# Transposing q and k of batches 1 to 3 by VectorE in 32x32 blocks, on data loaded as runs of 32 values

## Chip, cores and metric

One core of a Trainium2 chip. The metric is the device time of one execution in microseconds (us), lower is better. Before the change it is 926.97 us, the median of three runs (926.3 to 927.1).

## What is computed

```python
def _attn_ref(q, k, v):                       # 4 batches, 8 heads, 576 tokens, head size 64
    scores = q @ k.T / 8
    # heads 0 to 3 see the last 32 tokens (local), heads 4 to 7 every 32nd token before (strided)
    attn = softmax(where(mask, scores, -1e9))
    return attn @ v

def reference(...):
    x = attn_out.transpose(0, 2, 1, 3).reshape(2304, 512)
    h = relu(x @ w_in)                        # 512 -> 2048
    x = (s * h * h + b) @ w_out               # 2048 -> 512
    return ((x @ w_a) * (x @ w_b)) @ w_o2     # 512 -> 1536 -> 512
```

All inputs and the output are float32. The matmuls of the two MLPs run as three passes over a high and a low half of each operand (`PASSES`, line 153).

## The kernel before

**Chunks and steps.** The first MLP runs over five chunks of tokens, n = 0 to 4 (line 896). Chunk 0 holds the first 128 tokens of all four batches; chunk n from 1 on holds the other 448 tokens of batch n-1. A chunk takes 16 steps, one for each f of the 2048 hidden columns in blocks of 128. A step is, on TensorE, 12 matmuls `h` (`h_mm`, line 586), 12 matmuls `acc` for the f of two steps earlier (`o_mm`, line 614), and then a piece of the attention for the next chunk (`attend`, line 817). So TensorE sees `h`, `acc`, a short piece, `h`, `acc`, a short piece. After each `h`, ScalarE makes the ReLU and the high half of its square, VectorE the square and the low half (lines 599 to 610).

**The attention of the next chunk.** While chunk n-1 runs, the attention for chunk n is made by six generators: four `local` (line 238; two pairs of heads, each in a part of 4 and a part of 3 blocks of 64 tokens) and two `strided` (line 299; two pairs of heads). `plan` (line 804) says at which step each generator does its next part. For `local`: load q and k two steps ahead; transpose (step 0); load v, scores and first half of the softmax (step 1); second half (step 2); transpose the probabilities, `ppt` (step 3); multiply by v, `po`, and split the result into the halves of x (step 4). A `local` begins every 4 steps, so its step 0 falls together with step 4 of the one before. `strided` does the same over 8 steps, with the load three steps ahead.

**Transposes of q and k before.** Rows of 64 values are loaded, tokens on partitions (lines 249 and 307 to 311). TensorE transposes them against an identity into PSUM (`pst`, line 96, called from 259, 317 and 325), ScalarE copies PSUM into `qkT` or `sqkT` (lines 260, 318, 332). A `local` part of 4 blocks takes 5 such matmuls, a part of 3 blocks 4, a `strided` 10.

**Rooms.** `qkT` and the transposed probabilities `pT` share one buffer (tag `lT`), `sqkT` and `spT` another (tag `sT`); the loaded `sqk` shares a third with the probabilities `spt` (tag `sn`). Each has one buffer: the next user waits until the last reader is done.

**Order.** The order on each engine is set by a scheduler from the dependencies and its own simulation; TensorE's order is fixed by hand (`in_order`, line 85). All loads of the attention and of the weights go through the queue of SP, in order. The weights of the second MLP are converted meanwhile, a piece at a time (`convert_w2`, line 633, `raw`, lines 129 to 139).

The order of the passes matters at the first step of a chunk:

```python
for kk in range(KD):              # kk: block of 128 columns of x, blocks 0 and 1 from `local`
    for a, c in PASSES:           # ((0, 0), (0, 1), (1, 0)); c = 1 is the low half of x
        mm(ph, lhsT=wi[f][:, a, kk, :], rhs=x_t[n][:, c, kk, 0:T], ...)
```

Of the kernel before, what the change touches and what calls it, by code (L numbers as in the profile page):

```python
# [8 lines left out]
F32 = mybir.dt.float32  # L9
# [3 lines left out]
AF = mybir.ActivationFunctionType  # L13
# [5 lines left out]
P = 128  # L19
# [6 lines left out]
def sparse_attention_two_mlps(  # L26
# [14 lines left out]
    nc = tc.nc  # L41
    B, H, S, D = q.shape
# [3 lines left out]
    STR = 32  # L46
    HL = H // 2
# [24 lines left out]
    ps_a = ctx.enter_context(tc.tile_pool(name="ps_a", bufs=3, space=PSUM))  # L72
# [4 lines left out]
    sp = att.enter_context(tc.tile_pool(name="sp", bufs=1, side="right"))  # L77

    ident = const.tile([P, P], F32, name="ident")
# [15 lines left out]
    def mm_t(*args):  # L95
        last_pe[:] = [nc.tensor.transpose(*args).ins]  # L96
# [65 lines left out]
    QT = 64  # L162
    WK = QT + STR
    RG = 4
    NG = STR // RG
    NI = S // STR
    I0 = TF // STR
    IS = NI - QT // RG
    NK = NI * RG
# [64 lines left out]
    def window(src, bb, head, t0, nt):  # L234
        at = src[bb, head, t0:S, :]
        return bass.AP(at.tensor, at.offset, [[D, WK], [QT * D, nt], [1, D]])

    def local(bb, n, pair, t0, nt):

        nq, nk = nt * QT, nt * QT + STR  # L240
        mq, mk = (P, nk // 3) if nk % 3 == 0 else (nq // 2, nk // 2)
        cq, ck = nq // mq, nk // mk
        nu = -(-nt // 2)
        tl = lambda shape, name: lp.tile(shape, F32, tag=name, name=name)
        qn, kn = tl([P, 2, 2, D], "qn"), tl([P, 3, 2, D], "kn")
        for h in range(2):
            for dst, src, a, m in ((qn, q, t0, mq), (kn, k, t0 - STR, mk)):
                z = t0 + nq
                nc.sync.dma_start(
                    out=dst[:m, 0:(z - a) // m, h],  # L250
                    in_=src[bb, 2 * pair + h, a:z, :].rearrange("(c p) d -> p c d", p=m),
                )
        yield
        qkT = lp.tile([P, 9 * QT], F32, tag="lT", name="qkT")
        qT, kT = qkT[:, 0:nq], qkT[:, nq:nq + nk]
        for src, m, c, dst, eng in ((qn, mq, cq, qT, 0), (kn, mk, ck, kT, 0)):
            ps = ps_a.tile([P, c, m], F32, tag="a", name="pst")
            for i in range(c):
                mm_t(ps[:, i], src[:m, i].rearrange("p h d -> p (h d)"), ident[:m, :m])
            nc.scalar.activation(out=dst.rearrange("p (c m) -> p c m", m=m), in_=ps, func=AF.Copy)  # L260
        yield
        vn = tl([WK, 4, 2, D], "vn")
        for h in range(2):
            nc.sync.dma_start(out=vn[:, 0:nt, h], in_=window(v, bb, 2 * pair + h, t0 - STR, nt))
        pss = [ps_a.tile([P, nu, WK], F32, tag="a", name="pss") for _ in range(2)]

        def put(alone):
            for j in range(2 * nu if alone else nt):
                i = min(j, nt - 1) * QT
                for h in range(2):  # L270
                    hr = slice(h * D, (h + 1) * D)
                    mm(
                        pss[h][j % 2 * QT:(j % 2 + 1) * QT, j // 2],
                        lhsT=qT[hr, i:i + QT], rhs=kT[hr, i:i + WK],
                        start=alone, stop=(alone or j >= nt - 2),
                    )

        pt = tl([P, 2, nu, WK], "lpt")
        yield from softmax(pt, pss, lmask, put, n == 1)
        yield  # L280
        ppt = ps_a.tile([WK, 2 * nu, P], F32, tag="a", name="ppt")
        for i in range(2 * nu):
            mm_t(ppt[:, i, :], pt[:, i // nu, i % nu], ident)
        pT = lp.tile([WK, 2, nu * P], F32, tag="lT", name="pT")
        nc.scalar.activation(out=pT.rearrange("p h t -> p (h t)"), in_=ppt.rearrange("p i t -> p (i t)"), func=AF.Copy)
        yield
        po = ps_a.tile([P, nq], F32, tag="a", name="po")
        for j in range(nt):
            for h in range(2):
                mm(  # L290
                    po[h * D:(h + 1) * D, j * QT:(j + 1) * QT],
                    lhsT=vn[:, j, h, :], rhs=pT[:, h, j * QT:(j + 1) * QT],
                    start=True, stop=True,
                )
        xt, c0 = x_tile(n), t0 - TF
        split(xt[:, 0, pair, c0:c0 + nq], xt[:, 1, pair, c0:c0 + nq], po)
        yield

    def strided(bb, n, pair):

        NC, NH = (S - IS * STR) // P, 3
        MK = S // (2 * NH)
        room = sp.tile([P, NC + 2 * NH, 2, D], F32, tag="sn", name="sqk")
        sq, sk = room[:, 0:NC], room[:MK, NC:]
        for h in range(2):
            head = HL + 2 * pair + h
            nc.sync.dma_start(
                out=sq[:, :, h], in_=q[bb, head, IS * STR:S, :].rearrange("(c p) d -> p c d", p=P)
            )
            nc.sync.dma_start(  # L310
                out=sk[:, :, h], in_=k[bb, head].rearrange("(c p) d -> p c d", p=MK)
            )
        yield
        qkT = sp.tile([P, NG, QT + NK], F32, tag="sT", name="sqkT")
        ps = ps_a.tile([P, NC * P], F32, tag="a", name="pst")
        for c in range(NC):
            mm_t(ps[:, c * P:(c + 1) * P], sq[:, c].rearrange("p h d -> p (h d)"), ident)
        nc.scalar.activation(
            out=qkT[:, :, 0:QT].rearrange("p g (i r) -> p g i r", r=RG),
            in_=ps.rearrange("p (i g r) -> p g i r", r=RG, g=NG), func=AF.Copy,  # L320
        )
        for half in range(2):
            ps = ps_a.tile([P, NH * MK], F32, tag="a", name="pst")
            for c in range(NH):
                mm_t(
                    ps[:, c * MK:(c + 1) * MK], sk[:, half * NH + c].rearrange("p h d -> p (h d)"),
                    ident[:MK, :MK],
                )
            ih = NI // 2
            dst = qkT[:, :, QT:].rearrange("p g (r i) -> p g r i", r=RG)[:, :, :, half * ih:(half + 1) * ih]  # L330
            src = ps.rearrange("p (i g r) -> p g r i", r=RG, g=NG)
            nc.scalar.activation(out=dst, in_=src, func=AF.Copy)
        yield
        sv = sp.tile([NK, NG, 2, D], F32, tag="sv", name="sv")
        for h in range(2):
            vr = v[bb, HL + 2 * pair + h].rearrange("(i g r) d -> r i g d", r=RG, g=NG)
            for r in range(RG):
                nc.sync.dma_start(out=sv[r * NI:(r + 1) * NI, :, h], in_=vr[r])  # L338
        nu = NG // 2
        pss = [ps_a.tile([P, nu, NK], F32, tag="a", name="pss") for _ in range(2)]  # L340

        def put(alone):
            for g in range(NG):
                for h in range(2):
                    hr = slice(h * D, (h + 1) * D)
                    mm(
                        pss[h][g % 2 * QT:(g % 2 + 1) * QT, g // 2],
                        lhsT=qkT[hr, g, 0:QT], rhs=qkT[hr, g, QT:],
                        start=alone, stop=(alone or g >= NG - 2),
                    )  # L350

        pt = sp.tile([P, 2, nu, NK], F32, tag="sn", name="spt")
        yield from softmax(pt, pss, smask, put, False)
        yield
        skip = QT - IQ * RG
        pT = sp.tile([NK, 2, NG, IQ * RG], F32, tag="sT", name="spT")
        for h in range(2):
            ppt = ps_a.tile([NK, nu, 2, QT], F32, tag="a", name="ppt")
            for u in range(nu):
                mm_t(ppt[:, u].rearrange("p j t -> p (j t)"), pt[:, h, u], ident)  # L360
            src = ppt.rearrange("p u j t -> p (u j) t")[:, :, skip:]
            nc.scalar.activation(out=pT[:, h], in_=src, func=AF.Copy)
        yield
        po = ps_a.tile([P, TR], F32, tag="a", name="po")
        pg = po.rearrange("p (i g r) -> p g i r", r=RG, g=NG)
        for g in range(NG):
            for h in range(2):
                mm(
                    pg[h * D:(h + 1) * D, g], lhsT=sv[:, g, h],
                    rhs=pT[:, h, g].rearrange("p (i r) -> p i r", r=RG), start=True, stop=True,  # L370
                )
        xt = x_tile(n)
        split(xt[:, 0, HL // 2 + pair, 0:TR], xt[:, 1, HL // 2 + pair, 0:TR], po)
        yield
# [506 lines left out]
    for what in ORDER.split():  # L881
        name, of = what[:-1], int(what[-1])
# [104 lines left out]
    for pair in range(NP2):  # L987
        acc = [ps_acc.tile([P, DM], F32, tag="acc", name="acc2") for _ in range(TB2 // P)]
        later_x = []
        for g in range(NG2):  # L990
            i = pair * NG2 + g
# [112 lines left out]
```

## Time and profile before

| | us |
|---|---|
| median of 3 runs | 926.97 |
| the profiled execution, as timed | 926.5 |
| its span in the profile | 924.7 |
| TensorE matmul busy | 911.6 (99%) |
| VectorE busy | 615.5 (67%) |
| ScalarE busy | 418.5 (45%) |
| share of the span in the chain that ended last, TensorE | 89% |

The profile shows one execution. TensorE's busy time includes overlap of consecutive matmuls, so its starts are a better measure of a step than its durations. In the trace's timeline, a row merges equal instructions that follow each other: start, the time they cover, engine, line, operation, output and inputs, count. "Idle before" is the engine's idle time just before, with what ended it. Stage boundaries: chunk 1 begins at 138.4 us, chunk 2 at 233.9, chunk 3 at 328.7, chunk 4 at 422.9.

### The profile page before, as it was taken

To read this page: it belongs to the slowest core of one execution; us is meant where nothing else is said; L and a number is where in the kernel's file an instruction comes from. 1 tells how busy PE (TensorE), PEld (TensorE's weight loads), DVE (VectorE), ACT (ScalarE), POOL (GpSimd) and SP (SyncE) were. 2 spreads that over 40 slices of the span, in tenths; PEclk is the share of its full clock that TensorE was granted. 3 is DMA by queue.
4 is the path that set the end of the run, shared out by engine and by line. 5 is a ranking of instruction groups with operands and counts; after the bars stand their busy time and mean duration, and the time that the engine had idled before them with its cause. 6 is when DMAs were issued, how large, how long until landed. Compare 5 with 4: busy or idle time off the path is not lost.

```text
span 924.7 us, 14965 instructions
## 1 busy us (share of the span) xinstructions
PE 911.6 (99%) x5584; PEld 818.8 (89%) x5584; DVE 615.5 (67%) x1219; ACT 418.5 (45%) x882; POOL 40.0 (4%) x104
## 2 busy tenths in 40 slices
PE   8999999999999999999999999999999999999998
PEld 6777878988888888888999999998999998999986
DVE  6798974666675756664674867766766765776741
ACT  6687764433443444345323444444333444333322
POOL 3000000111000000000100000000000000000000
PEclk9999999999999999999999999999999999999999
DMA  9666523536554555535766643430623221423010
GB/s 235 191 209 200 191 59 116 149 107 180 173 146 130 146 176 146 149 103 186 237 211 216 191 129 121 136 101 27 227 86 107 87 86 44 139 86 114 29 35 35
DMA packets 127368, 125.63 MB, mean 136 GB/s; under 512 B 73024, under 2 KB 103232, under 8 KB 127296
## 3 DMA queue, kind: packets, MB, share of 16 engines
q1 hardware_dynamic: 120608, 108.43, 39.8%
q0 software_dynamic: 4608, 15.73, 4.4%
q8 instruction: 44, 0.72, 0.3%
q10 hardware_dynamic: 2080, 0.52, 0.3%
q14 instruction: 28, 0.23, 0.1%
HBM read 99.48 MB, written 25.17 MB: 135 GB/s over the span
## 4 chain that ended last, share of the span: by engine, by line
PE 89%; DVE 4%; SPq 3%; DMA 1%; ACT 1%; issue 1%; ACTq 0%; DVEq 0%
PE acc L93 35%; PE pp L93 27%; PE h L93 20%; PE po L93 2%; PE pst L96 2%; SPq L404 1%; PE ppt L96 1%; PE pss L93 1%; DMA raw<-in_moe_w_out_dram 1%; DVE raw L135 1%; DVE raw L139 1%; DVE w L111 1%; SPq L338 1%; DMA raw<-in_moe_w_in_dram 1%; DVE raw L132 0%
## 5 line engine op out<-in xcount | busy, mean ns | idle before, releaser
L93 PE MATMUL pp<-x2w,wf 128*128 128x384 f32 x1512 | 269.5, 336 | 0.3 <-ACT u L418 0.2
L93 PEld LDWEIGHTS pp<-x2w,wf 128*128 128x128 f32 x1512 | 263.6, 188 | 4.6 <-ACT u L418 1.4
L93 PE MATMUL h<-x,w 128*128 128x448 f32 (+1 forms) x960 | 219.8, 378 | 0.9 <-ACT r L599 0.9
L93 PE MATMUL acc<-gt,w 128*128 128x448 f32 (+2 forms) x960 | 212.7, 371 | 0.0
L93 PEld LDWEIGHTS acc<-gt,w 128*128 128x128 f32 x960 | 180.6, 188 | 19.4
L93 PEld LDWEIGHTS h<-x,w 128*128 128x128 f32 x960 | 175.4, 188 | 21.7 <-ACT r L599 1.2
L93 PE MATMUL acc<-o2w,abt 128*128 128x512 f32 x648 | 153.6, 391 | 0.0
L93 PEld LDWEIGHTS acc<-o2w,abt 128*128 128x128 f32 x648 | 121.3, 188 | 23.6
L599 ACT ACTIVATE r<-h 128x448 f32<-128x448 f32 (+1 forms) x80 | 44.4, 555 | 157.9 <-PE h L93 153.7
L609 DVE TENSOR_TENSOR r<-r 128x448 f32<-128x448 f32 x64 | 40.0, 625 | 103.4 <-ACT gt L608 103.3
L418 ACT ACTIVATE abt<-c 128x384 fp32r<-128x384 f32 x36 | 18.9, 526 | 91.4 <-DVE c L423 91.4
L423 DVE TENSOR_TENSOR wf<-w2r,wf 128x512 fp32r<-128x512 f32 x72 | 39.7, 552 | 22.0 <-ACT wf L418 22.0
L418 ACT ACTIVATE u<-pp 128x384 f32<-128x384 f32 x36 | 17.7, 492 | 78.9 <-PE pp L93 78.9
L418 ACT ACTIVATE wf<-w2t 128x512 fp32r<-128x512 f32 x72 | 45.1, 627 | 17.8 <-PE pp L93 17.2
L423 DVE TENSOR_TENSOR wf<-w2t,wf 128x512 fp32r<-128x512 f32 x72 | 49.3, 685 | 0.1
L423 DVE TENSOR_TENSOR c<-pp,u 128x384 f32<-128x384 f32 x36 | 20.0, 557 | 42.2 <-PE pp L93 42.2
L423 DVE TENSOR_TENSOR u<-pp,u 128x384 f32<-128x384 f32 x72 | 39.9, 554 | 9.3 <-PE pp L93 8.8
L135 DVE SCALAR_TENSOR_TENSOR raw<-raw 128x512 uint32<-128x512 uint32 x66 | 44.3, 688 | 0.5
L129 ACT ACTIVATE raw<-raw 128x512 f32<-128x512 f32 x66 | 42.6, 671 | 2.7 <-DMA raw<-in_moe_w_in_dram 2.0
L610 DVE TENSOR_TENSOR gt<-r,gt 128x448 fp32r<-128x448 f32 x64 | 40.0, 625 | 4.1
L418 ACT ACTIVATE wf<-w2r 128x512 fp32r<-128x512 f32 x72 | 37.2, 516 | 0.0
L423 DVE TENSOR_TENSOR abt<-dly,abt 128x384 fp32r<-128x384 f32 x36 | 20.0, 556 | 25.6 <-ACT abt L418 25.5
(133 smaller groups left out, 872.0 us busy)
## 6 DMA issues: line engine op xcount, KB each, us to landing
w2t<-w2s SPq DMA_DIRECT2D x36, 512.0 KB
w2r<-w2d SPq DMA_DIRECT2D x60, 256.0 KB
raw<-in_moe_w_out_dram SPq DMA_DIRECT2D x28, 512.0 KB
w2d<-w2s POOLq DMA_DIRECT2D x36, 256.0 KB, 4.4
raw<-in_moe_w_in_dram SPq DMA_DIRECT2D x16, 512.0 KB
raw<-in_moe_w_a_dram SPq DMA_DIRECT2D x12, 512.0 KB
raw<-in_moe_w_b_dram SPq DMA_DIRECT2D x12, 512.0 KB
w2s<-w2t POOLq DMA_DIRECT2D x12, 512.0 KB, 4.4
```

The costliest lines, as they stand in the source:

```text
L93: last_pe[:] = [nc.tensor.matmul(*args, **kwargs).ins]
L96: last_pe[:] = [nc.tensor.transpose(*args).ins]
L111: return nc.vector.tensor_tensor(out=lo, in0=src, in1=hi.bitcast(F32), op=ALU.subtract)
L129: nc.scalar.activation(out=high.bitcast(F32), in_=high.bitcast(F32), func=AF.Copy, scale=HIGH_SCALE)
L135: nc.vector.scalar_tensor_tensor(out=low, in0=high, scalar=3, in1=low, op0=ALU.logical_shift_left, op1=ALU.bitwise_or)
L139: nc.vector.scalar_tensor_tensor(out=out, in0=high, scalar=0x80000000, in1=low, op0=ALU.bitwise_and, op1=ALU.bitwise_or)
L338: nc.sync.dma_start(out=sv[r * NI:(r + 1) * NI, :, h], in_=vr[r])
L418: i = nc.scalar.activation(**kwargs).ins
L423: i = getattr(nc.vector, method)(**kwargs).ins
L599: relu = nc.scalar.activation(out=r, in_=ph, func=AF.Relu)
L609: nc.vector.tensor_tensor(out=r, in0=r, in1=r, op=ALU.mult)
L610: last = nc.vector.tensor_tensor(out=lo, in0=r, in1=hi.bitcast(F32), op=ALU.subtract)
```

## The change

For chunks 2 to 4 (batches 1 to 3), q and k are loaded in runs of 32 values: each load fills 32 partitions, so that 32x32 blocks lie in the partitions in which their transposes end. VectorE transposes all blocks of a `local` part in one instruction, those of a `strided` in two (q and k), and writes `qkT` or `sqkT` directly. The matmuls `pst` and ScalarE's copies of those batches go; batch 0 keeps them. A generator issues 8 loads for q and k where it issued 4, of 32 partitions each instead of 96 to 128, with the same bytes.

```diff
+    def blocks_load(room, first_, src, bb, head, a, z):
+        for h in range(2):
+            at = src[bb, head + h, a:z, :].rearrange("(j t) (e c) -> e t j c", t=STR, c=STR)
+            for e in range(D // STR):
+                p0 = h * D + e * STR
+                nc.sync.dma_start(
+                    out=room[p0:p0 + STR, first_:first_ + (z - a) // STR], in_=at[e]
+                )
     def local(bb, n, pair, t0, nt):
...
+        by_blocks = n > 1
+        if by_blocks:
...
+            blocks_load(qk, 0, q, bb, 2 * pair, t0, z)
+            blocks_load(qk, nq // STR, k, bb, 2 * pair, t0 - STR, z)
...
         qkT = lp.tile([P, 9 * QT], F32, tag="lT", name="qkT")
...
+        if by_blocks:
+            nc.vector.transpose(out=qkT[:, 0:nq + nk].rearrange("p (j c) -> p j c", c=STR), in_=qk)
+        else:
...
     def strided(bb, n, pair):
...
+            blocks_load(room, 0, q, bb, HL + 2 * pair, IS * STR, S)
+            blocks_load(room, NQ, k, bb, HL + 2 * pair, 0, S)
...
+        if by_blocks:
+            nc.vector.transpose(
+                out=qkT[:, :, 0:QT].rearrange("p g (i r) -> p i g r", r=RG), in_=room[:, 0:NQ]
+            )
+            nc.vector.transpose(
+                out=qkT[:, :, QT:].rearrange("p g (r i) -> p i g r", r=RG), in_=room[:, NQ:]
+            )
+        else:
+            strided_by_tensor(sq, sk, qkT, NC, NH, MK)
```

How the order moves, at three places. Line numbers of the changed kernel are up to 39 higher; its L648 and L649 are L609 and L610 of before, its L243 the loads of `blocks_load`, its L274 the transposition in `local`, its L364 and L367 those of q and k in `strided`.

On TensorE, the step of chunk 2 in which the first `strided` of chunk 3 was transposed (244.4 us in the trace). Before:

```order
L93 MATMUL acc<-gt,w 128x450 x12
L96 MATMUL pst<-ident,sqk 128x128 x4
L96 MATMUL pst<-ident,sqk 128x96 x6
L93 MATMUL h<-x,w 128x448 x12
L93 MATMUL acc<-gt,w 128x448 x12
L96 MATMUL ppt<-ident,lpt 96x128 x4
```

On TensorE, the same step in the changed kernel:

```order
L93 MATMUL acc<-gt,w 128x450 x12
L93 MATMUL h<-x,w 128x448 x12
L93 MATMUL acc<-gt,w 128x448 x12
L96 MATMUL ppt<-ident,lpt 96x128 x4
L93 MATMUL pss<-sqkT 64x72 x16
```

The ten transposes are gone and nothing takes their place; the rest of TensorE's order is the same from the first row to the last.

On VectorE, the end of chunk 1, where the last `local` of chunk 2 is split into x and the first `local` of chunk 3 is transposed (233.5 us). Before:

```order
L610 TENSOR_TENSOR gt<-r,gt 128x448
L132 TENSOR_SCALAR raw<-raw 128x512
L111 TENSOR_TENSOR x<-po,x 128x192
L135 SCALAR_TENSOR_TENSOR raw<-raw 128x512
L139 SCALAR_TENSOR_TENSOR w2s<-raw 128x512
```

On VectorE, the same place in the changed kernel:

```order
L649 TENSOR_TENSOR gt<-r,gt 128x448
L132 TENSOR_SCALAR raw<-raw 128x512
L274 STREAM_TRANSPOSE qkT<-qk 128x544
L111 TENSOR_TENSOR x<-po,x 128x192
L135 SCALAR_TENSOR_TENSOR raw<-raw 128x512
```

The transposition of the next chunk stands ahead of the low half of x (`x<-po,x`), which the first step of the new chunk reads. At the end of chunk 0 it stands there too, without the row of L132; at the end of chunk 2 as here.

On VectorE, chunk 2, around the end of the first `strided` of chunk 3 (274 to 282 us). Before:

```order
L135 SCALAR_TENSOR_TENSOR raw<-raw 128x512
L139 SCALAR_TENSOR_TENSOR w2s<-raw 128x512
L111 TENSOR_TENSOR x<-po,x 128x448
L609 TENSOR_TENSOR r<-r 128x448
L610 TENSOR_TENSOR gt<-r,gt 128x448
L111 TENSOR_TENSOR x<-po,x 128x256
```

On VectorE, the same stretch in the changed kernel:

```order
L135 SCALAR_TENSOR_TENSOR raw<-raw 128x512
L364 STREAM_TRANSPOSE sqkT<-sqk 128x16x8x4
L139 SCALAR_TENSOR_TENSOR w2s<-raw 128x512
L111 TENSOR_TENSOR x<-po,x 128x448
L367 STREAM_TRANSPOSE sqkT<-sqk 128x18x8x4
L648 TENSOR_TENSOR r<-r 128x448
L649 TENSOR_TENSOR gt<-r,gt 128x448
L274 STREAM_TRANSPOSE qkT<-qk 128x416
```

The second `strided`, which TensorE used to transpose at 291.9 us, is now transposed some three steps earlier, right behind the `po` of the first one. The queue of SP at this place, before:

```order
L117 DMA raw<-in_moe_w_b_dram 128x4x256
L307 DMA sqk<-in_q_dram 128x4x64
L310 DMA sqk<-in_k_dram 96x6x64
L307 DMA sqk<-in_q_dram 128x4x64
L310 DMA sqk<-in_k_dram 96x6x64
L122 DMA raw<-in_moe_w_out_dram 128x1024
```

The queue of SP at this place, in the changed kernel:

```order
L117 DMA raw<-in_moe_w_b_dram 128x4x256
L243 DMA sqk<-in_q_dram 32x16x32 x4
L243 DMA sqk<-in_k_dram 32x18x32 x4
L122 DMA raw<-in_moe_w_out_dram 128x1024
L377 DMA sv<-in_v_dram 18x8x64 x3
```

Eight loads of 32 partitions stand where four stood, between the same neighbours.

## Rows read from the trace of the kernel before

**Rows 1.** Windows: us, busy PE, PEld, DVE, ACT, POOL (count), PEclk, DMA share, GB/s

```profile
140.00:235.00 95.00, 95.00 (x701) 84.43 (x700) 58.31 (x119) 39.86 (x81) 10.82 (x25) 1.00 0.48 135
235.00:330.00 95.00, 95.00 (x705) 84.99 (x704) 62.29 (x130) 40.57 (x83) 7.02 (x13) 1.00 0.53 154
330.00:420.00 90.00, 90.00 (x669) 80.63 (x668) 58.73 (x120) 37.87 (x77) 7.02 (x13) 1.00 0.49 138
```

**Rows 2.** Timeline of PE, 242 to 264 us: start, us, engine, line, operation

```profile
244.44 1.09 PE L96 MATMUL pst<-ident,sqk 128*128 128x128 f32 x10
245.32 2.68 PE L93 MATMUL h<-x,w 128*128 128x448 f32 x12
...
257.14 0.44 PE L96 MATMUL pst<-ident,qn 128*128 128x128 f32 x2
...
257.61 2.68 PE L93 MATMUL h<-x,w 128*128 128x448 f32 x12
260.12 2.59 PE L93 MATMUL acc<-gt,w 128*128 128x448 f32 x12
```

**Rows 3.** Timeline of PE: a part of 3 blocks, then an `h` behind `po`

```profile
304.50 0.38 PE L96 MATMUL pst<-ident,qn 96*128 96x96 f32 x2
...
304.84 2.68 PE L93 MATMUL h<-x,w 128*128 128x448 f32 x12
307.36 1.99 PE L93 MATMUL acc<-gt,w 128*128 128x448 f32 x9
...
275.43 2.69 PE L93 MATMUL h<-x,w 128*128 128x448 f32 x12
277.96 2.59 PE L93 MATMUL acc<-gt,w 128*128 128x448 f32 x12
```

**Rows 4.** Timelines of PE, DVE and ACT where chunk 2 begins

```profile
233.44 0.44 PE L96 MATMUL pst<-ident,qn 128*128 128x128 f32 x2
...
233.91 2.68 PE L93 MATMUL h<-x,w 128*128 128x448 f32 x12
...
233.49 0.42 DVE L132 TENSOR_SCALAR raw<-raw 128x512 uint32<-128x512 uint32 x1
233.92 0.36 DVE L111 TENSOR_TENSOR x<-po,x 128x192 fp32r<-128x192 f32 x1
...
233.56 0.33 ACT L110 ACTIVATE x<-po 128x192 fp32r<-128x192 f32 x1 [1.38 <-PE po L93]
```

**Rows 5.** Groups of VectorE by form: count, busy us, mean ns, idle before

```profile
L221 DVE TENSOR_TENSOR spt<-spt,mx 128x576 f32<-128x576 f32 x8 | 6.1, 757 | 0.2
...
L132 DVE TENSOR_SCALAR raw<-raw 128x512 uint32<-128x512 uint32 x66 | 26.8, 423 | 0.0
...
L383 DVE CAST ident_b<-ident 128x128 bf16<-128x128 f32 x1 | 1.2, 1212 | 1.7 <-POOL ident masks.py:199 1.7
```

**Rows 6.** Timelines of SP's queue, DVE and PE around the second `strided` of chunk 3

```profile
269.16 0.37 SPq L307 DMA_DIRECT2D sqk<-in_q_dram  x1
...
271.38 0.35 SPq L122 DMA_DIRECT2D raw<-in_moe_w_out_dram  x1
...
274.93 0.69 DVE L135 SCALAR_TENSOR_TENSOR raw<-raw 128x512 uint32<-128x512 uint32 x1
...
279.34 0.63 DVE L609 TENSOR_TENSOR r<-r 128x448 f32<-128x448 f32 x1 [2.47 <-ACT gt L608]
...
286.48 0.56 PE L93 MATMUL pss<-qkT 64*64 64x96 f32 x16
```

**Rows 7.** DMA view, 228 to 234.5 (packets, MB, share), then 140 to 420 us

```profile
q1 hardware_dynamic: 936, 0.23, 15.7%
...
q1 hardware_dynamic: 52552, 30.35, 40.9%
...
w2d<-w2s POOLq DMA_DIRECT2D x36, 256.0 KB, 4.4
```

More of the change, by code (lines that the diff above doesn't have):

```diff
@@ L244, in local @@
         tl = lambda shape, name: lp.tile(shape, F32, tag=name, name=name)
[L245 to L252, printed above, removed]
+        qk = tl([P, 5, 2, D], "qk")
+        z = t0 + nq
+        by_blocks = n > 1
+        if by_blocks:
+            qk = qk.rearrange("p a h d -> p (a h d)")[:, 0:nq + nk]
+            qk = qk.rearrange("p (j c) -> p j c", c=STR)
+            blocks_load(qk, 0, q, bb, 2 * pair, t0, z)
+            blocks_load(qk, nq // STR, k, bb, 2 * pair, t0 - STR, z)
+        else:
+            qn, kn = qk[:, 0:2], qk[:, 2:]
+            for h in range(2):
+                for dst, src, a, m in ((qn, q, t0, mq), (kn, k, t0 - STR, mk)):
+                    nc.sync.dma_start(
+                        out=dst[:m, 0:(z - a) // m, h],
+                        in_=src[bb, 2 * pair + h, a:z, :].rearrange("(c p) d -> p c d", p=m),
+                    )
         yield
@@ L255, in local @@
         qT, kT = qkT[:, 0:nq], qkT[:, nq:nq + nk]
[L256 to L260, printed above, removed]
+        if by_blocks:
+            nc.vector.transpose(out=qkT[:, 0:nq + nk].rearrange("p (j c) -> p j c", c=STR), in_=qk)
+        else:
+            for src, m, c, dst in ((qn, mq, cq, qT), (kn, mk, ck, kT)):
+                ps = ps_a.tile([P, c, m], F32, tag="a", name="pst")
+                for i in range(c):
+                    mm_t(ps[:, i], src[:m, i].rearrange("p h d -> p (h d)"), ident[:m, :m])
+                nc.scalar.activation(out=dst.rearrange("p (c m) -> p c m", m=m), in_=ps, func=AF.Copy)
         yield
@@ L297, in local, with strided_by_tensor @@
         yield
[L299 to L314, printed above, removed]
+    def strided_by_tensor(sq, sk, qkT, NC, NH, MK):
         ps = ps_a.tile([P, NC * P], F32, tag="a", name="pst")
@@ L332, in strided @@
             nc.scalar.activation(out=dst, in_=src, func=AF.Copy)
+    def strided(bb, n, pair):
+        NC, NH = (S - IS * STR) // P, 3
+        MK = S // (2 * NH)
+        room = sp.tile([P, NC + 2 * NH, 2, D], F32, tag="sn", name="sqk")
+        by_blocks = n > 1
+        NQ = NI - IS
+        if by_blocks:
+            room = room.rearrange("p a h d -> p (a h d)")[:, 0:(NQ + NI) * STR]
+            room = room.rearrange("p (j c) -> p j c", c=STR)
+            blocks_load(room, 0, q, bb, HL + 2 * pair, IS * STR, S)
+            blocks_load(room, NQ, k, bb, HL + 2 * pair, 0, S)
+        else:
+            sq, sk = room[:, 0:NC], room[:MK, NC:]
+            for h in range(2):
+                head = HL + 2 * pair + h
+                nc.sync.dma_start(
+                    out=sq[:, :, h], in_=q[bb, head, IS * STR:S, :].rearrange("(c p) d -> p c d", p=P)
+                )
+                nc.sync.dma_start(
+                    out=sk[:, :, h], in_=k[bb, head].rearrange("(c p) d -> p c d", p=MK)
+                )
+        yield
+        qkT = sp.tile([P, NG, QT + NK], F32, tag="sT", name="sqkT")
+        if by_blocks:
+            nc.vector.transpose(
+                out=qkT[:, :, 0:QT].rearrange("p g (i r) -> p i g r", r=RG), in_=room[:, 0:NQ]
+            )
+            nc.vector.transpose(
+                out=qkT[:, :, QT:].rearrange("p g (r i) -> p i g r", r=RG), in_=room[:, NQ:]
+            )
+        else:
+            strided_by_tensor(sq, sk, qkT, NC, NH, MK)
         yield
```

## The prediction

> **What bounds the kernel now.** I read the windows first, then TensorE's timeline, then those of VectorE, ScalarE and SP at the places where the order moves. The windows over chunks 1 to 3 show TensorE busy for every microsecond, 95.00 of 95, 95.00 of 95 and 90.00 of 90, at a granted clock of 1.00, the upper of its two levels (2.4 GHz), while VectorE works 58 to 62 us of 90 to 95 and ScalarE some 40 [rows 1]. So in this stretch, which holds nearly all that the change touches, time is what TensorE has to do: a matmul taken from its queue shortens the run, and work given to VectorE costs nothing until TensorE waits for it. The rest of the kernel is the same program and moves as a whole.
>
> **What goes from TensorE.** I count from start to start, since durations overlap. A `strided` spends 245.32 - 244.44 = 0.88 us on its ten transposes [rows 2]. A `local` part of 4 blocks spends 257.61 - 257.14 = 0.47, one of 3 blocks 304.84 - 304.50 = 0.34 [rows 2, 3]. What follows hardly changes: `h` to `acc` takes 260.12 - 257.61 = 2.51 or 307.36 - 304.84 = 2.52 us behind transposes and 277.96 - 275.43 = 2.53 behind `po`, as it will stand now [rows 2, 3]. So 0.02 and 0.01 come back: 0.45 and 0.33 net. Each of the three batches has two of each: 3 x 2 x (0.88 + 0.45 + 0.33) = **10.0 us** less. ScalarE loses its copies out of PSUM as well, which is worth nothing, because TensorE doesn't wait for it in these windows; PSUM gets freer, worth nothing for the same reason.
>
> **What VectorE gets.** 24 transpositions: 12 of a `local` (544 or 416 columns) and 12 of a `strided` (512 and 576). No row shows this operation. Nearest is a float32 instruction of 576 columns, 0.757 us, or 1.31 ns a column [rows 5]; I take that, as the blocks are read and written a value at a time too: 0.72 us for 544 columns, 0.55 for 416. The lower end is the cheapest operation per column, 512 in 0.423 us, so 0.45 for 544; the upper end is the longest VectorE instruction of the whole trace, 1.21 us [rows 5]. In sum about 16 us (10 to 29) over 280 us, of which VectorE has some 100 idle [rows 1]. Cover for it is the slack between a `qkT` and the scores that read it, one step later; gone, each late microsecond would be TensorE's. Two places are tight.
>
> **Place one: the first step of a chunk.** The transposes were also a pause in which the new x was finished. At the start of chunk 2, TensorE's `po` ends at 233.44; ScalarE writes the high half from 233.56 to 233.89, VectorE the low half from 233.92 to 234.28, and `h` begins only at 233.91 [rows 4]. Its fifth matmul is the first to read that low half. Now `h` begins at 233.44, and, at 2.51/12 = 0.21 us each, the fifth at 234.28. VectorE does the instruction of L132 until 233.91, then, by the new order, the transposition until 234.63, then the low half in 0.36: 234.99. TensorE waits 0.7 us. Chunk 3 begins alike; at the start of chunk 1 the 0.42 us of L132 aren't in between, so 0.3. Sum 1.7 us lost; with 0.45 us for a transposition 0.9, with 1.21 us 3.2.
>
> **Place two: the early transposition of the second `strided`.** VectorE works in order, and L364 and L367 wait for loads. SP begins the loads at 269.16, when the room comes free, and issued the next transfer at 271.38 [rows 6]. Eight loads at 0.5 us occupy SP until 273.2; over three batches SP issues 72 more of them, which delays the neighbours by about 2 us each time. L364 is reached at 275.6, when L135 ends [rows 6] and `po` has freed the room of `sqkT`; L367 about 277.6, behind L364, L139 and x. The load is 2 x 2 x (512 + 576) = 4352 packets of 128 bytes, twice as many as before at half the size. A packet of 256 bytes took 0.157 x 16 x 6.5 us / 936 = 17.4 ns of a DMA engine; all of q1 in the three chunks, at 578 bytes a packet, 0.409 x 16 x 280 / 52552 = 34.9 ns [rows 7]. A line through both gives 10 ns at 128 bytes. I take 17.4, the nearest size, and keep 10 and 34.9. The last landing is at most 269.2 + 4.4 (issue to landing of a 256 KB transfer [rows 7]) + 4352 x 17.4 ns / 16 = 278.3, so L367 waits under 1 us. Behind it stand r and gt (0.63 each; gt is needed two steps later) and the transposition of 416 columns, which the scores need at 286.48, or 286.1 without the transposes between [rows 6]. Counted back, 286.1 - 0.57 - 1.26 - 0.76 = 283.5: **a landing up to 283.5 costs nothing**, and at 34.9 ns it comes at 283.1. So I put this at zero. The loads of `local` are issued some 20 us ahead, with half the packets, and need nothing.
>
> The Trainium skill speaks against such loads: "DMA: Bandwidth & Descriptors", Specifications, has 512 bytes as the least transfer for line rate, and its Bandwidth section calls transfers under 64 KB descriptor-dominated. The 17.4 ns agree in kind: 256 bytes in 17.4 ns is 14.7 GB/s for an engine, below the page's 27 GiB/s. By the page the price per packet might not fall with size, which the sum already assumes; that it rises is the third rival.
>
> **Sum.** 926.5 (the execution profiled) - 10.0 + 1.7 = 918.2. That execution lies 0.5 below the median of the runs, 926.97, so I say **918.7** for a median. From the bounds of the transposition: 917.9 to 920.2. I widen it to 916.9 (no wait at chunk starts) and 921.2, for waits of some tenths that no row shows.
>
> **The rivals.**
>
> *Part of it is lost in VectorE's queue (about 923).* If packets cost 39 ns, the second place lands at 269.2 + 4.4 + 10.6 = 284.2, 0.7 us late, six times: 4.2 us back, 922.9. For it: DMA share is already 0.48 to 0.53 [rows 1] and two weight loads of 512 KB are in flight at that moment. Against it: the four loads of before were issued 20 us ahead of use and 39 is over twice the row of the nearest size.
>
> *No change: the time moves into another wait of TensorE.* ScalarE would have to be the next bound, with `h`'s single PSUM bank waiting for its ReLU. ScalarE is idle more than half of each window [rows 1] and gets less to do. Against it, too, that nothing in the order of TensorE replaces the transposes. About 927.
>
> *Slower: the loads hold VectorE.* The mechanism is place two with a dearer packet. If a packet of 128 bytes costs three times the row, 52 ns, the landing is at 269.2 + 4.4 + 14.1 = 287.7, 4.2 us behind 283.5; six `strided` lose 25 us, and the time is 926.97 - 8.3 + 25.2 = 943.9. It decides from 8.3/6 = 1.4 us late, that is from 41.5 ns. For it: every load now writes only 32 partitions, which no row shows, and the order puts the wait ahead of work that TensorE needs. Against it: 41.5 ns is 2.4 times the price of a packet twice as large.
>
> *The change doesn't do what it says.* That is excluded for the transposes: the order shows them gone.
>
> **How the numbers follow.** A run of this kernel tells 0.2%, 1.9 us, from no change. Forecast, 916.9 to 921.2: 0.66. Better than 916.9: 0.03, since the ten microseconds are all that TensorE gives back. Partly lost, 921.2 to 925.1: 0.13. No change: 0.06. Slower: 0.12, most of it at the loads. Faster is then 0.82, same 0.06, slower 0.12. For 8 in 10 I take the forecast, most of the better case and the nearer part of the partly lost: 916.5 to 923.5.
>
> **What would show it.** In the windows of chunks 1 to 3 TensorE stays busy throughout, each `strided` step shorter by 0.88 us, `acc` followed by `h` at once. At each chunk start TensorE's fifth `h` matmul waits some tenths for `x` of VectorE. Transpositions of 544 columns take about 0.7 us. L364 and L367 show waits on `sqk` loads of under 1 us, and the scores behind them begin at once. DMA share goes from 0.5 to about 0.6 (8192 packets of q and k a batch become 16384, so 24576 more x 17.4 ns / 16 = 27 us over 280). I am wrong if TensorE waits for `qkT`, or for `gt` behind a VectorE that waits for DMA, by over a microsecond a time, or if a transposition takes several microseconds.

## The result and the profile after

The changed kernel takes **917.9 us** (median of four runs, 917.05 to 919.16) against 926.68 for the kernel before in the same comparison: a ratio of 0.9906, 95% interval 0.9889 to 0.9923. The forecast was 918.7. The execution profiled is the longest of the four: 919.16 us, span 917.5.

The page's line of busy times, and its line of queue q1:

```profile
PE 903.5 (98%) x5470; PEld 808.5 (88%) x5470; DVE 631.8 (69%) x1243; ACT 404.1 (44%) x840; POOL 40.3 (4%) x104
q1 hardware_dynamic: 146336, 108.43, 41.1%
```

The windows of chunks 1 to 3, with the columns of [rows 1]:

```profile
140.00:235.00 95.00, 94.58 (x675) 83.23 (x675) 64.33 (x128) 35.08 (x68) 11.54 (x26) 1.00 0.53 139
235.00:330.00 95.00, 94.73 (x693) 83.67 (x692) 68.73 (x140) 36.76 (x71) 7.15 (x14) 1.00 0.59 158
330.00:420.00 90.00, 90.00 (x645) 80.14 (x645) 62.20 (x126) 35.67 (x69) 6.48 (x12) 1.00 0.55 160
```

TensorE is still busy throughout, but for short pauses at the starts of the chunks. VectorE has 3.5 to 6.4 us more per window, ScalarE 2 to 5 less, the DMA engines 5 to 6 points more.

I measure the change from mark to mark: from the last `po` of chunk 0 to the last `po` before chunk 4, both short rows of TensorE that all kernels have. Before, these start at 137.42 and 422.44, **285.02 us** apart; now at 138.49 and 415.10, **276.61**: 8.41 less, where the steps of the prediction say 10.0 - 1.7 = 8.3. Outside the marks the profiled execution loses 1.07 us ahead of the first one, in chunk 0, which the change doesn't touch (last section), and 0.14 behind the last one, so its span is 7.2 us shorter.

**Where it came from.** TensorE at the place of [rows 2], now (start, duration, engine, line, operation):

```profile
240.31 2.60 PE L93 MATMUL acc<-gt,w 128*128 128x450 f32 x12
242.74 2.64 PE L93 MATMUL h<-x,w 128*128 128x448 f32 x12
```

`acc` takes 2.43 us from start to start, and `h` follows at once; the 0.88 us of ten transposes are gone.

**Where some of it went back.** TensorE, then VectorE, at the start of chunk 2, the place of [rows 4]:

```profile
231.11 0.57 PE L93 MATMUL po<-pT,vn 96*64 96x64 f32 x12
231.61 1.08 PE L93 MATMUL h<-x,w 128*128 128x448 f32 x4
233.03 1.89 PE L93 MATMUL h<-x,w 128*128 128x448 f32 x8 [0.33 <-DVE x L111]
234.75 1.59 PE L93 MATMUL acc<-gt,w 128*128 128x450 f32 x7
```

```profile
231.66 0.43 DVE L132 TENSOR_SCALAR raw<-raw 128x512 uint32<-128x512 uint32 x1
231.99 0.74 DVE L274 STREAM_TRANSPOSE qkT<-qk 128x544 f32<-128x544 f32 x1
232.65 0.32 DVE L111 TENSOR_TENSOR x<-po,x 128x192 fp32r<-128x192 f32 x1
```

Four matmuls of `h` run, the fifth waits for the low half of x, which stands behind the transposition. From `h` to `acc` it is 3.14 us here, 2.91 in chunk 1 and 3.07 in chunk 3. A step without a pause takes 2.53 [rows 3], so 0.38 + 0.61 + 0.54 = **1.53 us** are lost.

**Place two.** VectorE, SP and TensorE around the early transposition of the second `strided`, the place of [rows 6]:

```profile
272.52 0.71 DVE L364 STREAM_TRANSPOSE sqkT<-sqk 128x512 f32<-128x512 f32 x1
...
274.97 1.26 DVE L367 STREAM_TRANSPOSE sqkT<-sqk 128x576 f32<-128x576 f32 x1 [0.63 <-DMA sqk<-in_k_dram]
...
278.19 0.61 DVE L274 STREAM_TRANSPOSE qkT<-qk 128x416 f32<-128x416 f32 x1 [0.58 <-PE po L93]
```

```profile
266.14 2.00 SPq L243 DMA_DIRECT2D sqk<-in_q_dram  x4
268.18 2.47 SPq L243 DMA_DIRECT2D sqk<-in_k_dram  x4
```

```profile
283.22 0.56 PE L93 MATMUL pss<-qkT 64*64 64x96 f32 x16
```

The eight loads are issued over 4.5 us, the last lands 4.3 us later, and VectorE waits 0.63 us: the only such wait among the six `strided`. The scores at 283.22 wait for nothing.

### The profile page after: what moved, and what is told of

The parts are those of the page before. It is cut to its first block, busy times and chain, and to the rows that moved or that the text cites. A ratio compares the mean times of both kernels' runs of the same rounds, so it can differ in the third digit from the quotient of the medians.

```text
span 917.5 us, 14789 instructions
## 1 busy us (share of the span) xinstructions
PE 903.5 (98%) x5470; PEld 808.5 (88%) x5470; DVE 631.8 (69%) x1243; ACT 404.1 (44%) x840; POOL 40.3 (4%) x104
## 4 chain that ended last, share of the span: by engine, by line
PE 90%; DVE 5%; ACT 2%; DMA 2%; issue 1%; SPq 0%; ACTq 0%; DVEq 0%
PE acc L93 36%; PE pp L93 28%; PE h L93 21%; PE po L93 2%; PE ppt L96 1%; PE pss L93 1%; DMA raw<-in_moe_w_in_dram 1%; DMA fqk<-in_k_dram 1%; PE fpo L93 1%; DVE w L111 1%; DVE raw L135 1%; DVE raw L139 1%; DVE raw L132 0%; ACT fpt L457 0%; DVE gt L111 0%
## 5 line engine op out<-in xcount | busy, mean ns | idle before, releaser
L93 PE MATMUL h<-x,w 128*128 128x448 f32 (+1 forms) x960 | 222.2, 380 | 1.9 <-ACT r L638 1.2
L93 PEld LDWEIGHTS acc<-gt,w 128*128 128x128 f32 x960 | 180.4, 188 | 19.9
L648 DVE TENSOR_TENSOR r<-r 128x448 f32<-128x448 f32 x64 | 40.0, 625 | 82.1 <-ACT gt L647 81.9
L135 DVE SCALAR_TENSOR_TENSOR raw<-raw 128x512 uint32<-128x512 uint32 x66 | 44.1, 685 | 0.4
L649 DVE TENSOR_TENSOR gt<-r,gt 128x448 fp32r<-128x448 f32 x64 | 39.7, 620 | 4.3 <-DVE r L648 0.5
```

The lines of the kernel that those rows point to most:

```text
L93: last_pe[:] = [nc.tensor.matmul(*args, **kwargs).ins]
L135: nc.vector.scalar_tensor_tensor(out=low, in0=high, scalar=3, in1=low, op0=ALU.logical_shift_left, op1=ALU.bitwise_or)
L648: nc.vector.tensor_tensor(out=r, in0=r, in1=r, op=ALU.mult)
L649: last = nc.vector.tensor_tensor(out=lo, in0=r, in1=hi.bitcast(F32), op=ALU.subtract)
```

## The experiments

All kernels below are the changed kernel with one edit. The scheduler orders each of them anew, so an edit can move other rows too; where that counts, it is said. "Stretch" is the time from mark to mark; it has little of the scatter of whole runs (276.61 and 276.57 us in two profiles of the changed kernel).

### Is it TensorE's time?

**Strided heads alone.** In `local`, `by_blocks = False`.

> The changed kernel with the blocks of 32x32 in the strided heads alone; the local splits go over TensorE as before. My theory (the gain is TensorE's time): six strided pairs at 0.88 us give 5.3 us less than before, about 921.4 us (ratio 0.9943), and no pause between the rows `h` at the starts of chunks 1 to 3, since no local transposition stands in front of the low half of x. Rival (the gain comes from ScalarE, which copies the strided transposes at high cost in the gap before the scores, and not from TensorE): nearly the whole gain is here, about 918 us.

Measured: 921.33 us, ratio to before 0.995 (0.9931 to 0.9969); stretch 279.45, that is 5.57 below before. The steps from `h` to `acc` at the starts of chunks 1 to 3 are 2.51 us each: no pause. As my theory has it.

**Local parts alone.** In `strided`, `by_blocks = False`.

> The changed kernel with the blocks of 32x32 in the local splits alone; the strided heads go over TensorE as before. My theory: six splits at 0.45 and six at 0.33 give 4.7 us less, the starts of chunks 1 to 3 take back 1.5, so about 923.5 us (ratio 0.9966), and the steps from `h` to `acc` there stay at 2.9 to 3.1 us. Rival (ScalarE's relief): within 1 us of the kernel before, since only the small copies are gone.

Measured: 923.41 us, ratio 0.9973 (0.9962 to 0.9983); stretch 282.20, 2.82 below before, with `h` to `acc` at 2.89, 3.14 and 3.07. The two parts add up: 5.57 + 2.82 = 8.39 of the 8.41.

**Both engines transpose.** The matmuls are put back as idle work:

```diff
+    def again(room, cols, groups):
+        flat = room.rearrange("p j c -> p (j c)")
+        for m, c in groups:
+            ps = ps_a.tile([P, c, m], F32, tag="a", name="pst")
+            for i in range(c):
+                a = min(i * P, cols - P)
+                mm_t(ps[:, i], flat[:m, a:a + P], ident[:m, :m])
...
+            again(qk, nq + nk, ((mq, cq), (mk, ck)))
...
+            again(room, (NQ + NI) * STR, ((P, NC), (MK, NH), (MK, NH)))
```

> The changed kernel, in which VectorE transposes and its results are used, and TensorE does in addition as many transposing matmuls of the same shapes into the same PSUM buffers as before the change; their results are not read (they are redundant, and transpose other data), and ScalarE copies nothing. My theory (what was gained is TensorE's own time in a stretch where it is busy throughout): the 10 us come back and the pause at the chunk starts stays, so 926 to 928 us, ratio about 1.000. Rival (the gain came from ScalarE's copies, which no longer hold PSUM buffers and the scores): the time stays near 918 us.

Measured: 926.72 us, ratio 1.0003 (0.9994 to 1.0013); stretch 285.30. The gain is gone although ScalarE still has no copies to make: its windows show 35.03, 35.60 and 33.56 us. So the gain was the matmuls. One part I had wrong: the pause doesn't stay. The first `h` of chunk 2 comes behind 0.47 us of transposes:

```profile
233.41 0.69 PE L96 MATMUL pst<-ident,qk 128*128 128x128 f32 x5
233.88 2.86 PE L93 MATMUL h<-x,w 128*128 128x448 f32 x12
236.58 2.60 PE L93 MATMUL acc<-gt,w 128*128 128x450 f32 x12
```

`h` to `acc` takes 2.70 here, 2.50 and 2.60 in chunks 1 and 3. The transposes fill the time in which VectorE makes the low half late.

### Is the pause at the chunk starts only an order?

```diff
-            nc.vector.transpose(out=qkT[:, 0:nq + nk].rearrange("p (j c) -> p j c", c=STR), in_=qk)
+            with after(list(last_lo)):
+                nc.vector.transpose(out=qkT[:, 0:nq + nk].rearrange("p (j c) -> p j c", c=STR), in_=qk)
...
-        split(xt[:, 0, pair, c0:c0 + nq], xt[:, 1, pair, c0:c0 + nq], po)
+        last_lo[:] = [split(xt[:, 0, pair, c0:c0 + nq], xt[:, 1, pair, c0:c0 + nq], po).ins]
```

> The changed kernel, with one edit: the transposition of q and k of a local split waits in VectorE's order until the low half of x of the split before it has been written. My theory: the stall of 0.3 us between two rows `h` at the start of chunks 1 to 3 (1.53 us in all in the changed kernel's profile, from the first `h` to its `acc`, over the same steps of the kernel before) comes from that one order, VectorE working 0.74 us at the transposition while the low half waits. Then the step from `h` to `acc` falls back from 2.9 to 3.1 us to about 2.5 at each of the three starts, and the time is 1.0 to 1.5 us below the changed kernel, about 916.5 us (ratio 0.989). Rival: the stall comes from the split as such, which ScalarE and VectorE finish one after the other, and the transposition stands there by chance: then the steps stay near 3.0 us and the time stays at 917.9.

VectorE and TensorE at the start of chunk 2 in this kernel (its L275 is L274 of the changed kernel):

```profile
230.58 0.36 DVE L111 TENSOR_TENSOR x<-po,x 128x192 fp32r<-128x192 f32 x1
230.85 0.73 DVE L275 STREAM_TRANSPOSE qkT<-qk 128x544 f32<-128x544 f32 x1
```

```profile
230.10 2.77 PE L93 MATMUL h<-x,w 128*128 128x448 f32 x12
232.71 2.60 PE L93 MATMUL acc<-gt,w 128*128 128x450 f32 x12
```

Measured: 916.08 us, ratio to before 0.9896 (0.9876 to 0.9915); stretch 275.36, 1.25 below the changed kernel. `h` to `acc` takes 2.65, 2.61 and 2.61: the pauses are gone and 0.1 us each is left. Since the medians of two comparisons differ by less than their intervals are wide, I ran both kernels once more, side by side:

> The changed kernel itself, beside the next one on the same chip: 917 to 918.5 us by every theory.

> The kernel with the transposition behind the low half of x, once more, beside the changed kernel on the same chip. My theory (1.2 us of pause at three chunk starts are gone): 1.0 to 1.5 us below the changed kernel. Rival (the difference of the first comparison, 1.8 us between medians of four runs each, was chance): within 0.5 us of it.

Measured: the changed kernel 918.32 us, ratio 0.9914 (0.9900 to 0.9929), stretch 276.57; the reordered one 916.66, ratio 0.9893 (0.9877 to 0.9910), stretch 275.35. The intervals of the ratios overlap, so the times alone wouldn't settle it; that the stretch shortens by 1.25 and 1.22 us in two profiles, with the pauses gone at the three places, does. This is the version that beats both.

### What is VectorE's work worth?

Each transposition stands in a `for _ in range(2):`.

> The changed kernel with each of VectorE's transpositions done twice, the same values written again: 20 us more of VectorE over the stretch of 280 us. My theory (VectorE has some 90 us idle there, and its work costs only where TensorE waits for it): the pause at the starts of chunks 1 to 3 grows by 0.74 us each, 2.2 us in sum, elsewhere nothing: about 920 us. Rival (VectorE's slack is used up in the places between a transposition and its scores, and every further microsecond is late): 925 us or more.

Measured: 919.29 us, ratio 0.9921 (0.9905 to 0.9938); stretch 277.27, only 0.66 above the changed kernel. By their groups the transpositions take 39.6 us in place of 19.9. The windows show VectorE at 69.94, 73.44 and 65.39 us, 13.5 more in sum: they count the overlap of neighbouring rows once, and begin behind the first transpositions. Of the three pauses that I named only one grew: in `local`, the scheduler put the second transposition behind the low half of x, as at the start of chunk 1:

```profile
138.69 0.74 DVE L275 STREAM_TRANSPOSE qkT<-qk 128x544 f32<-128x544 f32 x1 [0.51 <-PE po L93]
139.36 0.32 DVE L111 TENSOR_TENSOR x<-po,x 128x192 fp32r<-128x192 f32 x1
139.60 0.72 DVE L275 STREAM_TRANSPOSE qkT<-qk 128x544 f32<-128x544 f32 x1
```

The 0.66 lies almost whole at the start of chunk 3 (`h` to `acc` 3.71 in place of 3.07), where the doubled transposition of k in `strided` stands ahead of x on VectorE. So 20 us more of VectorE cost 0.7, nearly all of it at the one place where more of its work stands ahead of x.

### What does the write pattern cost?

The transposition of k took 1.25 us for 576 columns, where the others take 1.4 ns a column. It writes every value 18 words from the last; q's is written in runs of 4. The edit writes k in runs too, and the scores read it with the stride:

```diff
-                out=qkT[:, :, QT:].rearrange("p g (r i) -> p i g r", r=RG), in_=room[:, NQ:]
+                out=qkT[:, :, QT:].rearrange("p g (i r) -> p i g r", r=RG), in_=room[:, NQ:]
...
-                        lhsT=qkT[hr, g, 0:QT], rhs=qkT[hr, g, QT:],
+                        lhsT=qkT[hr, g, 0:QT],
+                        rhs=(qkT[hr, g, QT:].rearrange("p (i r) -> p r i", r=RG) if n > 1 else qkT[hr, g, QT:]),
```

> The changed kernel, in which the transposition of k of a strided pair writes runs of 4 consecutive values, as that of q does, and the scores read k with the stride instead (moving operand of `pss`). My theory: that transposition takes 1.25 us in place of 0.8 because it writes each value 18 words from the last; with runs of 4 the 576 columns take 0.80 us. The time does not change (917 to 918.5), since nothing waits for VectorE there. Rival: its price comes from its 576 columns or from the read, and stays 1.25 us. Open for both is whether `pss` reads slower with a stride (0.56 us for 16 matmuls now).

The groups of the changed kernel's transpositions (columns as in [rows 5]), then line 367 in this kernel (shortest, median and longest in ns):

```profile
L367 DVE STREAM_TRANSPOSE sqkT<-sqk 128x576 f32<-128x576 f32 x6 | 7.5, 1248 | 0.6 <-DMA sqk<-in_k_dram 0.6
L274 DVE STREAM_TRANSPOSE qkT<-qk 128x544 f32<-128x544 f32 x6 | 4.5, 743 | 0.5 <-PE po L93 0.5
L364 DVE STREAM_TRANSPOSE sqkT<-sqk 128x512 f32<-128x512 f32 x6 | 4.3, 712 | 2.0 <-PE po L93 2.0
L274 DVE STREAM_TRANSPOSE qkT<-qk 128x416 f32<-128x416 f32 x6 | 3.6, 606 | 0.6 <-PE po L93 0.6
```

```profile
L367 DVE STREAM_TRANSPOSE sqkT<-sqk x6: 735/752/778, 133.1 to 366.5; 128x576 f32<-128x576 f32 x6
```

The write pattern is the price: 752 ns against 1248. But the time is 921.48 us, ratio 0.9948 (0.9933 to 0.9963), not the 917 to 918.5 that I expected, and the stretch 279.60, 2.99 longer. TensorE pays for the stride. The scores of a `strided`, first in the changed kernel, then here:

```profile
155.94 0.73 PE L93 MATMUL pss<-sqkT 64*64 64x72 f32 x32
```

```profile
154.86 1.25 PE L93 MATMUL pss<-sqkT 64*64 64x72 f32 x32
```

Six times 0.52 is 3.1 us. VectorE's half microsecond was free, TensorE's isn't.

### What do the loads cost: packets, or SP's issuing?

**Runs of 16 values.**

```diff
-                nc.sync.dma_start(
-                    out=room[p0:p0 + STR, first_:first_ + (z - a) // STR], in_=at[e]
-                )
+                for c in (slice(0, STR // 2), slice(STR // 2, STR)):
+                    nc.sync.dma_start(
+                        out=room[p0:p0 + STR, first_:first_ + (z - a) // STR, c], in_=at[e][:, :, c]
+                    )
```

> The changed kernel with all loads of its blocks cut in two: runs of 16 values (64 bytes) in place of 32, twice as many transfers and packets for the same bytes. In the changed kernel's profile the loads of `sqk` at its early transposition are issued from 266.14 to 270.65 us, the last lands at 274.9, and the transposition of 416 columns behind it has to be done by the scores at 283.22: counted back by 0.61 + 1.26 + 1.25, a landing up to about 280 costs nothing. My theory: sixteen issues of 0.5 us end 3.6 us later, and the 4352 further packets at 5.6 ns on 16 engines (worked out from the shares of q1 before and after the change) add 1.5 us: landing at about 280, at the edge, so 918 to 920 us, a longer wait of VectorE for `sqk` (about 5 us in place of 0.6 at that place), and little of it on TensorE. Rival (a packet keeps its price as it gets smaller, 11.5 ns or more, and 4352 more take 3 us or more; the chunks' weights come late as well): the wait reaches TensorE at most of the six strided pairs, 923 us or more.

Measured: 927.5 us, ratio 1.0013 (1.0003 to 1.0024); stretch 284.26, 7.65 longer. The time is the rival's. But the place is not: 6.6 of the 7.65 us lie in chunk 3, at its start. SP, ScalarE, VectorE and TensorE there (its L368 is L367):

```profile
319.66 4.99 SPq L244 DMA_DIRECT2D sqk<-in_k_dram  x8
324.76 0.51 SPq L122 DMA_DIRECT2D raw<-in_moe_w_out_dram  x1
```

```profile
328.90 0.68 ACT L129 ACTIVATE raw<-raw 128x512 f32<-128x512 f32 x1 [5.73 <-DMA raw<-in_moe_w_out_dram]
329.48 0.31 ACT L110 ACTIVATE x<-po 128x192 fp32r<-128x192 f32 x1
```

```profile
327.19 1.26 DVE L368 STREAM_TRANSPOSE sqkT<-sqk 128x576 f32<-128x576 f32 x1 [3.41 <-DMA sv<-in_v_dram]
331.04 0.35 DVE L111 TENSOR_TENSOR x<-po,x 128x192 fp32r<-128x192 f32 x1
```

```profile
324.84 0.87 PE L93 MATMUL h<-x,w 128*128 128x448 f32 x3
329.84 0.74 PE L93 MATMUL h<-x,w 128*128 128x448 f32 x1 [4.13 <-ACT x L110]
331.44 3.21 PE L93 MATMUL h<-x,w 128*128 128x448 f32 x8 [0.86 <-DVE x L111]
```

Two waits meet here. A weight load for the second MLP is queued behind sixteen loads of `sqk`. ScalarE, in order, waits for it, and the high half of x stands behind, done at 329.8. VectorE's transposition of k waits 3.41 us for its loads (the view names a load of `sv`, but the transposition reads `sqk` alone). From then on VectorE works without a gap, the scheduler has put one more row (L135, 0.65 us) ahead of x, and the low half comes only at 331.04. This wait ends last: by these rows TensorE's fifth matmul would begin at 331.44 with the high half in time, too. At the start of chunk 2 ScalarE is in time, and VectorE's wait alone costs 0.97 us. VectorE's waits for the loads (17.5 us over six transpositions of k) cost TensorE little anywhere else.

**The same packets, twice the transfers.** Each load is cut by blocks in place of by columns: `for j0, j1 in ((0, nj // 2), (nj // 2, nj))`.

> The changed kernel with each load of its blocks cut into two transfers of half as many blocks: the packets stay as they are in the changed kernel (128 bytes, the same number), only the transfers that SP issues double, as in the run with runs of 16 values (927.5 us). My theory (in that run it was SP's time for issuing, some 0.5 to 0.6 us for each transfer, that made the weight loads queued behind it late, and not the packets, which the share of q1 prices at 4 to 6 ns each): this kernel is as slow as that one, 926 to 929 us, with TensorE waiting again at the starts of chunks 2 and 3. Rival (the packets of 64 bytes were the cause): about 918 us, as the changed kernel.

Measured: 922.91 us, ratio 0.9964 (0.9951 to 0.9977); stretch 280.53, 3.92 longer, all of it in chunk 3 again. Packets are nearly the same, 148640 on q1 against 146336. The time lies between the two expectations: twice the transfers, without smaller packets, give 3.92 of the 7.65. The rows show the same two waits, 4.9 us earlier on SP, so shorter at their end (its L245 are the loads, L369 is L367):

```profile
315.68 4.08 SPq L245 DMA_DIRECT2D sqk<-in_k_dram  x8
319.88 0.39 SPq L122 DMA_DIRECT2D raw<-in_moe_w_out_dram  x1
```

```profile
322.66 1.26 DVE L369 STREAM_TRANSPOSE sqkT<-sqk 128x576 f32<-128x576 f32 x1 [2.46 <-DMA sqk<-in_k_dram]
```

```profile
324.84 0.47 PE L93 MATMUL h<-x,w 128*128 128x448 f32 x1 [0.55 <-ACT x L110]
326.91 3.35 PE L93 MATMUL h<-x,w 128*128 128x448 f32 x8 [1.61 <-DVE x L111]
```

TensorE waits 0.55 us for ScalarE, behind the weight load, and then 1.61 for VectorE, whose transposition of k waits 2.46 for its loads. So the longer part is the loads that hold VectorE, and some 0.6 of it is again the row of L135 ahead of x.

An issue has a median of 453 ns for `sqk` of k here and 496 with runs of 16, so the sixteen of a `strided` explain some 0.7 us of SP's 4.9. Why SP falls the rest behind is not settled. What is shown: the packets themselves are cheap for the DMA engines. 51456 more of them raise q1 from 0.411 x 917.5 to 0.423 x 925.1 us, 14.2 us on 16 engines, 4.4 ns each; from mark to mark, 45149 more raise it from 0.452 x 276.61 to 0.500 x 284.26, 6.1 ns each. Whether smaller packets slow SP down is not shown.

**Batch 0 too.** `by_blocks = True` in both generators.

> The changed kernel with the blocks for batch 0 too, whose attention runs before and in chunk 0, where TensorE waits for ScalarE and VectorE (in the changed kernel the row `ppt` at 70.49 us waits 1.44 us for ScalarE). My theory (the change pays only where TensorE is the bound, and there by its transposes alone): batch 0's two strided pairs and four local ones save TensorE at most 3.3 us, but much of it in stretches in which it idles, and VectorE gets 6 us more in a stretch where it is late: between 916.5 and 920 us. Rival (every transpose taken from TensorE shortens the run): 914.6 us. Second rival (the small packets delay the weights that arrive in the first 60 us): over 921 us.

Measured: 925.80 us, ratio 0.9993 (0.9982 to 1.0004), the second rival's time. The stretch is 276.55, as in the changed kernel: all is lost ahead of the first mark, which comes 7.43 us later. It is lost at two places. The first `h` begins at 37.97 us in place of 31.64, mainly since VectorE waits for the loads of blocks, and `fxn`, the attention's output for chunk 0, which TensorE transposes next (`fpx`), stands behind:

```profile
31.71 0.74 DVE L274 STREAM_TRANSPOSE qkT<-qk 128x544 f32<-128x544 f32 x1 [6.18 <-DMA sqk<-in_q_dram]
32.46 1.23 DVE L462 TENSOR_TENSOR fxn<-fpo,sm 128x512 f32<-128x512 f32 x2
```

```profile
33.75 1.82 PE L96 MATMUL fpx<-ident,fxn 128*128 128x128 f32 x8 [4.79 <-DVE fxn L462]
```

The third `h` begins at 52.82 in place of 41.12. SP, ScalarE and TensorE there:

```profile
45.76 0.46 SPq L117 DMA_DIRECT2D raw<-in_moe_w_in_dram  x1
```

```profile
49.55 0.66 ACT L129 ACTIVATE raw<-raw 128x512 f32<-128x512 f32 x1 [4.24 <-DMA raw<-in_moe_w_in_dram]
```

```profile
52.82 5.33 PE L93 MATMUL h<-x,w 128*128 128x512 f32 x12 [8.14 <-ACT w L110]
```

The weight load that stands at 45.76 here stands at 39.46 in the changed kernel: SP is 6.3 us behind after the additional loads. ScalarE waits for it, and the weights `w` of the third `h` come behind that wait, at 52.13, where the changed kernel's ScalarE makes them ahead of it, at 37.80. So the weights are late, as that rival says, but by SP's issuing and by the order on ScalarE; that the small packets did it is not shown. VectorE's wait for the loads, about half of what is lost up to there, stands in none of the three expectations.

## Why the prediction was right

- **What bounds the kernel.** Right: with the transposes back and ScalarE's copies still gone, the gain is gone (926.72 us against 926.28 for the kernel before, stretch 285.30 against 285.02).
- **What goes from TensorE**, 10.0 us. Right: mark to mark 8.41 plus 1.53 lost at the chunk starts is 9.94. By parts, 5.57 against 6 x 0.88 = 5.3 for `strided`, and 2.82 + 1.5 = 4.3 against 4.7 for `local`.
- **Place one**, 0.3 + 0.7 + 0.7 = 1.7 us. Right in place, cause and size: 0.38 + 0.61 + 0.54; the run with the order turned round gives 1.25 back.
- **What VectorE gets.** 544 columns in 743 ns (0.72 said), 416 in 606 (0.55). The term that was mis-sized is the transposition of k in `strided`: 1.25 us, not 0.757, and above the upper end of 1.21 that I had taken from the longest row of the trace. All told 19.9 us, not 16. It lay where VectorE was idle. I looked at how the transposition reads, and not at how it writes. The Trainium skill has this in "Vector Engine (DVE) Microarchitecture Reference", Measured stream behaviour on trn2: a port keeps its rate only for runs of at least two adjacent words, and in the XOR program measured there a destination written in single words that step apart takes 1.71 to 2.51 ns a column. The rows of this transposition agree in kind: 1248 / 576 = 2.17, against 752 / 576 = 1.31 in runs of four.
- **Place two**, zero. Right: the loads landed 8.8 us after the first issue, where I had said 9.1 at most, and VectorE waited 0.63 us, where I had said under 1. That the two sums lie so near is in part luck: mine has 4.7 us of packets and 4.4 of landing, the rows show 4.5 of issuing and then 4.3 to the last landing. The packets were priced too high. The 25728 more raise q1 by (0.411 x 917.5 - 0.398 x 924.7) x 16 = 145 us on the whole span, 5.6 ns for each additional one, and by 5.4 and 5.6 from mark to mark in two profiles of the changed kernel. Two packets of 128 bytes then cost 17.4 + 5.6 ns where one of 256 cost 17.4, so one costs about 11.5, an estimate, near the 10 of my line through two sizes, which I had set aside. (The 0.57 us that I counted back for 416 columns should be my own 0.55; the 283.5 stays.) The forecast DMA share of 0.6 came out as 0.53 to 0.59.
- **The third rival**, loads that hold VectorE, had the danger right and its place and price wrong. It counted every late microsecond six times, and asked for dearer packets. In the changed kernel it did not come. In the runs with cut loads VectorE did wait at every transposition of k, 11.6 us and 17.5 us in all, and TensorE lost time at one or two of the six places: at the start of a chunk, the one step where TensorE reads x at once and VectorE makes its low half behind that wait. What made the loads late was SP, which issued them late; how far the smaller packets stand behind that in the run with runs of 16 is open. The same queue made a weight load late, and with it the high half of x on ScalarE. I had counted SP's issues (2 us a time) and looked for no reader of the weights behind them.

## What to carry to other kernels

Where TensorE is busy throughout a stretch, moving work from it pays its start-to-start time in full, if the new place is off its path; look then at the few steps where the removed work had been a pause, and put the new work behind what the next step reads. A load cut into smaller pieces was paid for on the issuing queue here: by the engine that waits in order for the last piece and has other work behind it, and by whatever is queued behind the load, weights included. The DMA engines' own time for the packets was small. An awkward stride belongs on the engine that has time: here the half microsecond was free on VectorE and cost 3 us on TensorE.

## What I had not expected of the hardware

**TensorE's clock fell in chunk 0 in some executions, at a pause that was there before.** Behind pauses of 0.6 and 1.4 us for the softmax, at 68 to 70.5 us, the granted clock stays 1.00 in the profile of before and in five others; in the changed kernel's two profiles and in those of four experiments it drops to the lower of its two levels (1.2 GHz) for a few microseconds, a mean of 0.69 over the stretch shown (0.50 from 72 to 74 us in the changed kernel). The windows, before and then after (the clock is the third number from the end):

```profile
70.50:76.00 5.50, 5.50 (x28) 4.55 (x26) 5.50 (x13) 4.79 (x12) 0.00 (x0) 1.00 0.72 194
```

```profile
70.50:76.00 5.50, 5.50 (x20) 4.43 (x21) 5.50 (x13) 3.21 (x10) 0.00 (x0) 0.69 0.66 179
```

Twelve matmuls `h` take 4.58 us there in place of 3.00. These 1.58 us more than cover the 1.07 lost ahead of the first mark. They are likely a part of why runs of one kernel scatter by 2 us: of the kernel before, six executions with a mean clock of 0.997 take 927.4 us in the mean and fifteen with 1.000 take 926.0, which does not show at which place the clock fell. The change did not cause the pause, and I can't say what decides whether the clock falls. In the run with twice the transfers it fell behind the stall at the start of chunk 3, where eight matmuls took 3.35 us in place of 1.89: a stall of 2.2 us cost 3.6. It fell there in the run with runs of 16, too (3.21 us for the eight).

**SP's time per transfer.** A load of 32 partitions, 24 to 72 KB, keeps SP's queue 0.44 to 0.50 us in the median. The Trainium skill, "DMA: Bandwidth & Descriptors", Issuing engines are not separate DMA queues, calls the time to initiate a transfer usually small against the transfer. For one load that holds here, 0.5 us against the 4.3 from issue to landing; but the eight of a `strided` took 4.5 us to issue and the last landed 4.3 us after, so together it was the half.
